# A grouped 1x1 convolution on one core: other ring sizes, slots of unequal size, a longer TensorE loop

## The chip, the core and the metric

The kernel runs on one core of one Trainium2 chip. The metric is device time in microseconds of one execution, the median of several runs; lower is better. A profiled execution gives a page and a trace, in which times count from the start of its span.

## The reference

The image has 512 x 512 pixels of 192 channels in bf16. The channels form 4 groups of 48, and each group is multiplied by a 48 x 48 matrix of its own, pixel by pixel (the window is 1 x 1, so there is no padding):

```python
xg = xp.reshape(B, H, W, G, Cg)                              # G = 4, Cg = 48
out = out + jnp.einsum('bhwgc,gcd->bhwgd', xg, w[0, 0])
return out.reshape(B, H, W, C)                               # C = 192
```

Input and output are 100.7 MB each, and every byte is moved once.

## The kernel before

**Columns and groups.** The 262,144 pixels are dealt to 128 partitions, 2,048 to each. One *column* is one pixel in each of the 128 partitions (384 bytes a partition). Four columns are a *group* (the `g` of the code), and there are 514 groups, 2 more than 512, because two short fields use fewer partitions. Two groups are a *pair*: 257 pairs.

**Fields.** `plan_fields` cuts the pixels into fields of consecutive pixels. In a full field (`FULL`) each of the 128 partitions holds one run of pixels. Two fields of 48 columns (`PARTIAL`, `UNEVEN`) are moved by five smaller transfers, two from SP or ACT and three from GpSimd, so that the DMA engines get unequal shares. In these fields 120 of the 128 rows are moved; in `UNEVEN` the first block also has 16 columns less. GpSimd issues small filler transfers (`filler`) ahead of two of its three.

**Rings.** Input lands in `ring`, 240 columns in three slots of 80. Results stand in `oring`, 280 columns, from which they are stored. `plan_pieces` lists the loads (pieces), at most a slot long; the first ones are `HEAD`, 8, 24 and 48 columns. `plan_stores` lists the stores, which end at the columns of `OGRID`, 72 or 68 columns apart, and get shorter at the end (`LATE_PART`, `LAST_PARTS`). A *unit* is one or more pieces that TensorE waits for together, at the first group of the unit.

**The work on a pair.** TensorE transposes the pair (12 transposes, L350) from `ring` to PSUM; VectorE copies it to one of `NXS` = 3 buffers `xT_sb` (L409); TensorE multiplies it by block-shaped weights (12 matmuls, L370); ScalarE copies each group to `oring` (L446) and issues the stores (L427). TensorE goes one pair ahead with its transposes: `step(pair)` is `transposes(pair + 1)`, then `matmuls(pair)`. Its program is unrolled in part: `loop_spans` finds a stretch of regular units, and a loop of 60 groups (30 pairs) runs 8 times; before it stand 9 pairs, after it 8.

**What orders the work.**
- SP goes through the pieces in order. Before a piece it waits until TensorE has transposed the groups whose columns the piece overwrites (`freed`, semaphore `t_done`), then it issues (L320). GpSimd does its parts of the two partial fields in the same way (L289 to L300), and tells TensorE when such a unit has landed.
- VectorE waits for the transposes of its pair and, because of its buffers, for the matmuls of `NXS` pairs before.
- ScalarE waits for the matmuls of its group; it issues a store when its last group is done; and before it writes columns of `oring` it waits for the landing of the store that read them before (`landed`, L420).

Of the kernel before, what the change touches and what calls it, by code (L numbers as in the profile page):

```python
# [1 line left out]

# [19 lines left out]
ESHIFT = 112  # L22
ECOLS = 272

BIG = 80
SLOTS = 3
RCOLS = SLOTS * BIG
OGRID = (72, 140, 212, 280)
OCOLS = OGRID[-1]
HEAD = (8, 24, 48)  # L30
LATE_COLS = 240
LATE_PART = 40
LAST_PARTS = (24, 20, 16, 8)
NXP = 4
NXS = 3
NOB = 4
NTOK = 6

FULL = (("sync", 0, 128, 128, 0),)

PARTIAL = (
    ("sync", 0, 16, 4, 0), ("sync", 32, 16, 4, 0),
    ("pool", 52, 44, 11, 0), ("pool", 20, 12, 3, 0), ("pool", 96, 32, 8, 0),
)
UNEVEN = (("sync", 0, 16, 4, 16), *PARTIAL[1:])
FRONT = ((6, ((48, PARTIAL), (32, FULL))), (11, ((48, UNEVEN), (32, FULL))))

FILL_ROWS = 5
FILL_BEFORE = (2, 3)


class Field:


    def __init__(self, cols, blocks, g0, pix):
        self.cols, self.g0, self.g1 = cols, g0, g0 + cols // 4
        self.full = blocks is FULL
        self.blocks = []
        for (queue, r0, rows, outer, less) in blocks:
            self.blocks.append((queue, r0, rows, outer, pix, cols - less))  # L60
            pix += rows * (cols - less)
        self.pix_end = pix
        assert cols % 4 == 0


class Piece:

    def __init__(self, i, field, c0, size):
        self.i, self.field = i, field
        self.c0, self.c1, self.size = c0, c0 + size, size  # L70
        self.g0, self.g1 = field.g0 + self.c0 // 4, field.g0 + self.c1 // 4
        self.at = 4 * self.g0 % RCOLS
        self.full, self.blocks = field.full, field.blocks
        assert size % 4 == 0 and self.at + size <= RCOLS

# [7 lines left out]

def plan_fields(npix):

    parts, head = [], sum(HEAD)
    for slots, special in FRONT:
        parts += [(head + BIG * slots, FULL), *special]
        head = 0
    cols = npix - sum((n - b[4]) * b[2] for n, blocks in parts for b in blocks)  # L90
    if cols < 128 * BIG:
        parts, cols = [], npix
    assert cols % 512 == 0
    fields, g, pix = [], 0, 0
    for n, blocks in [*parts, (cols // 128, FULL)]:
        fields.append(Field(n, blocks, g, pix))
        g, pix = fields[-1].g1, fields[-1].pix_end
    assert pix == npix
    return fields


def plan_pieces(fields):
    pieces = []
    for f in fields:
        first = [f.cols]
        if f.full:
            first = list(HEAD) if not f.g0 and sum(HEAD) <= f.cols else []
        c = 0
        while c < f.cols:
            n = first.pop(0) if first else min(BIG, f.cols - c)  # L110
            pieces.append(Piece(len(pieces), f, c, n))
            c += n
    return pieces


def plan_stores(fields):
    total = 4 * fields[-1].g1
    stores, at = [], 0
    for f in fields:
        c = 0  # L120
        if not f.full and at + f.cols > OCOLS:
            at = 0
        ends = []
        if f is fields[-1] and f.cols > LATE_COLS:
            ends = [f.cols - sum(LAST_PARTS[i:]) for i in range(len(LAST_PARTS))]
        while c < f.cols:
            if f.full:
                end = min([g for g in OGRID if g > at + 24] or [OCOLS]) - at + c
                if f.cols < BIG:
                    end = min(OCOLS - at + c, f.cols)  # L130
                if ends and c >= f.cols - LATE_COLS:
                    end = min(OCOLS - at, LATE_PART) + c
                end = min([end, f.cols] + [e for e in ends if e > c])
            else:
                end = f.cols
            stores.append(Store(f, c, end, at))
            c, at = end, (at + end - c) % OCOLS
    return stores


class Unit:


    def __init__(self, pieces):
        self.pieces, self.g0, self.g1 = pieces, pieces[0].g0, pieces[-1].g1
        self.slot = pieces[0].at // BIG
        self.regular = pieces[0].at % BIG == 0 and 4 * (self.g1 - self.g0) == BIG


def plan_units(pieces):  # L150
    units, rest = [], list(pieces)
    while rest:
        n = 1
        if rest[0].g0 and rest[0].at % BIG == 0:
            while n < len(rest) and rest[n].at % BIG:
                n += 1
        units.append(Unit(rest[:n]))
        rest = rest[n:]
    return units


def loop_spans(units):

    body, out, run = RCOLS // 4, [], []
    for u in units + [None]:
        if u and u.regular:
            run.append(u)
            continue
        if run:

            first = max((run[0].g0 - 1) // 2, 1)
            rounds = (run[-1].g1 - 2 * first - 2) // body
            if rounds > 1:
                out.append((first, body // 2, rounds))
        run = []
    return out


def bass_standalone__grouped__vision_kernel(nc, x, w, out):
# [11 lines left out]
    NG = pieces[-1].g1  # L191
    NP = (NG + 1) // 2
    LOOPS = loop_spans(units)
    assert all(RCOLS // 4 % n == 0 for n in (2 * NXS, 2 * NTOK, NXP))

# [4 lines left out]
    def groups(pair):  # L200
        return range(2 * pair, min(2 * pair + 2, NG))

    def transfers(ap, tile, part, queues):
        f, c0, c1, at = part.field, part.c0, part.c1, part.at
        for n, (queue, r0, rows, outer, pix, cols) in enumerate(f.blocks):
            if queue not in queues:
                continue
            px = ap[pix:pix + rows * cols, :]
            if f.full:
                view = px.rearrange("(p i) n -> p (i n)", p=rows)[:, c0 * C:c1 * C]  # L210
            else:
                assert (c0, c1) == (0, f.cols)
                view = px.rearrange("(c a i) n -> a c (i n)", a=outer, c=rows // outer)
            yield n, view, tile[r0:r0 + rows, at * C:(at + (c1 - c0 if f.full else cols)) * C]
# [12 lines left out]
    with ExitStack() as es:  # L227
        block = es.enter_context(nc.Block())
        ring = es.enter_context(nc.sbuf_tensor("ring", [128, RCOLS * C], BF16))
        oring = es.enter_context(nc.sbuf_tensor("oring", [128, OCOLS * C], BF16))  # L230
        xT_sb = [es.enter_context(nc.sbuf_tensor(f"xT_sb{i}", [128, 4 * UC], BF16)) for i in range(NXS)]
        ident = es.enter_context(nc.sbuf_tensor("ident", [128, 128], BF16))
# [7 lines left out]
        def sem(name):  # L240
            return es.enter_context(nc.semaphore(name))
# [6 lines left out]

        e_done = [sem(f"e_done{i}") for i in range(NTOK)]
        fa_done = [sem(f"fa_done{i}") for i in range(2 * NTOK)]  # L250
        fin = sem("fin")
# [3 lines left out]
        def columns(g):  # L255
            at = 4 * g % RCOLS
            return ring[:, at * C:(at + 4) * C]
# [11 lines left out]
        def _(gp):  # L269
# [12 lines left out]
            def filler():  # L282
                k = len(used)
                src = xf[0:2 * FILL_ROWS, 0:4].rearrange("(t p) n -> p t n", t=2)
                dst = fill[:, 8 * k:8 * k + 8].rearrange("p (t n) -> p t n", t=2)
                gp.dma_start(dst, src).then_inc(fill_sem[k], 16)  # L286
                used.append(k)

            for nth, u in enumerate(mixed):  # L289
                part = [p for p in u.pieces if not p.full]  # L290
                for p in part:
                    gp.wait_ge(t_done, freed(p))
                    for n, dram, sbuf in transfers(xf, ring, p, ("pool",)):
                        if n in FILL_BEFORE:
                            filler()
# [6 lines left out]
                for i, s in enumerate(stores):  # L302
                    if any(s.field is p.field for p in part):
                        for n, dram, sbuf in transfers(of, oring, s, ("pool",)):
                            if n in FILL_BEFORE:
                                filler()
# [16 lines left out]
        def _(pe):  # L323
# [12 lines left out]
            def transposes(pair):  # L336
                todo = []
                for g in groups(pair):
                    u = unit_of[g]
                    if g % 2 and pair:  # L340
                        pe.wait_ge(e_done[(pair - 1) % NTOK], 1)
                    if g == u.g0:
# [14 lines left out]
            def matmuls(pair):  # L357
                if pair + 1 == NP or len(groups(pair + 1)) < 2:
                    pe.wait_ge(e_done[pair % NTOK], 1)
                for g in groups(pair):  # L360
                    xs = xT_sb[pair % NXS][:, g % 2 * 2 * UC:(g % 2 + 1) * 2 * UC]
                    if g >= 2:
                        pe.wait_ge(fa_done[(g - 2) % (2 * NTOK)], 1)
                    last = None
# [35 lines left out]
        def _(dve):  # L400
            dve.wait_ge(wb_sem, 1)
            dve.tensor_copy(wt[:], o_ps[:, NOB - 1, 0:WCOLS]).then_inc(wc_sem, 1)  # L402
            for pair in range(NP):
                n = len(groups(pair))
                b0 = pair * 2 % NXP
                dve.wait_ge(t_done, pair + 1)
                if pair >= NXS:
                    dve.wait_ge(mm_done, 2 * (pair - NXS + 1))
                dve.tensor_copy(xT_sb[pair % NXS][:, 0:n * 2 * UC].rearrange("p (g c) -> p g c", g=n),  # L409
                                xT_ps[:, b0:b0 + n, 0:2 * UC]).then_inc(e_done[pair % NTOK], 1)  # L410
# [70 lines left out]
```

## Time and profile before

| | |
|---|---|
| median of 5 runs | 477.93 us (477.24 to 478.76) |
| the profiled execution | 477.8 us, span 476.1 us |
| PE busy, DVE busy, ACT busy | 90%, 52%, 82% of the span |
| bytes moved, mean rate | 201.57 MB, 423 GB/s |
| ScalarE's copy L446, VectorE's copy L409 | 801 ns x514, 958 ns x257 |
| SP's waits for TensorE (L320) | 397.9 us in 25 waits |
| ACT's waits for landed stores | 17.0 us in 8 waits |

The page cuts the span into 40 slices and gives each engine's busy share of a slice in tenths. The row DMA is the mean share of 16 DMA engines, and PEclk is the granted clock of TensorE in tenths. The chain is followed back from the last instruction, at each step to what released it. A row of the timeline has the start, the length, the engine, the line and, in brackets, the idle time before it with what ended it.

### The profile page before, as it was taken

To read this page: it belongs to the slowest core of one execution; us is meant where nothing else is said; L and a number is where in the kernel's file an instruction comes from. 1 tells how busy PE (TensorE), PEld (TensorE's weight loads), DVE (VectorE), ACT (ScalarE), POOL (GpSimd) and SP (SyncE) were. 2 spreads that over 40 slices of the span, in tenths; PEclk is the share of its full clock that TensorE was granted. 3 is DMA by queue.
4 is the path that set the end of the run, shared out by engine and by line. 5 is a ranking of instruction groups with operands and counts; after the bars stand their busy time and mean duration, and the time that the engine had idled before them with its cause. 6 is when DMAs were issued, how large, how long until landed. Compare 5 with 4: busy or idle time off the path is not lost.

```text
span 476.1 us, 13580 instructions
## 1 busy us (share of the span) xinstructions
PE 429.9 (90%) x6178; PEld 388.4 (82%) x6178; DVE 246.7 (52%) x258; ACT 388.5 (82%) x515; POOL 12.5 (3%) x28
## 2 busy tenths in 40 slices
PE   5999999999698999999997996899978969999991
PEld 4988889888697898888896896888878868988880
DVE  2555555555354555555553553555545535555550
ACT  2898899988587998988896885899878948988882
POOL 1000000200002000000000000200002000000000
PEclk9999999999999999999998998999999979999997
DMA  8999999999999999999999999999999999999997
GB/s 326 436 399 423 439 426 430 430 423 431 441 430 423 440 419 439 439 430 425 424 431 442 434 430 425 431 426 443 428 426 428 430 425 427 431 428 435 418 424 298
DMA packets 10674, 201.57 MB, mean 423 GB/s; under 512 B 2112, under 2 KB 2112, under 8 KB 2752
## 3 DMA queue, kind: packets, MB, share of 16 engines
q1 hardware_dynamic: 4320, 97.44, 48.0%
q10 hardware_dynamic: 5120, 97.42, 47.8%
q0 software_dynamic: 1216, 6.49, 3.3%
q8 instruction: 9, 0.15, 0.1%
q14 instruction: 9, 0.07, 0.0%
HBM read 100.68 MB, written 100.66 MB: 423 GB/s over the span
## 4 chain that ended last, share of the span: by engine, by line
PE 47%; DMA 39%; ACT 9%; issue 1%; another core or an unknown queue 1%; ACTq 1%; SPq 0%; POOLq 0%
DMA out_dram<-oring 30%; PE o_ps L370 27%; PE xT_ps L350 20%; DMA ring<-in_x_dram 9%; ACT oring L446 9%; ACTq L427 1%; SPq L320 0%; SPq L313 0%; ACTq L420 0%; POOLq L300 0%; POOLq L299 0%; ACTq L429 0%
## 5 line engine op out<-in xcount | busy, mean ns | idle before, releaser
L446 ACT CAST oring<-o_ps 128x768 bf16<-128x768 f32 x514 | 387.2, 801 | 77.7 <-PE o_ps L370 54.2
L409 DVE COPY xT_sb<-xT_ps 128x1536 bf16<-128x1536 bf16 x257 | 246.1, 958 | 214.1 <-PE xT_ps L350 214.1
L370 PE MATMUL o_ps<-wt,xT_sb 128*128 128x144 bf16 (+1 forms) x3084 | 289.2, 237 | 26.5 <-ACT oring L446 21.0
L370 PEld LDWEIGHTS o_ps<-wt,xT_sb 128*128 128x128 bf16 x3084 | 212.3, 99 | 65.0 <-ACT oring L446 55.9
L350 PE MATMUL xT_ps<-ident,ring 128*128 128x128 bf16 x3084 | 221.6, 222 | 6.7 <-POOLq L300 3.7
L350 PEld LDWEIGHTS xT_ps<-ident,ring 128*128 128x128 bf16 x3084 | 189.1, 99 | 9.5 <-POOLq L300 3.9
L286 POOL DMA_DIRECT2D fill<-in_x_dram x8 | 4.6, 573 | 349.1 <-PE xT_ps L350 234.5
L296 POOL DMA_DIRECT2D ring<-in_x_dram x6 | 3.3, 560 | 0.0
L307 POOL DMA_DIRECT2D out_dram<-oring x6 | 3.3, 555 | 0.0
L332 PE MATMUL o_ps<-w_sb,esel 48*128 48x48 bf16 x10 | 0.6, 210 | 2.8 <-DMA w_sb<-in_w_dram 2.8
L332 PEld LDWEIGHTS o_ps<-w_sb,esel 48*128 48x128 bf16 x10 | 0.5, 111 | 2.7 <-issue 2.7
L402 DVE CAST wt<-o_ps 128x480 bf16<-128x480 f32 x1 | 0.7, 657 | 3.3 <-PE o_ps L332 3.3
L446 ACT ACT_TABLE_LOAD x1 | 1.3, 1283 | 0.8 <-PEq L466 0.8
L273 POOL TENSOR_SCALAR_AFFINE_SELECT esel<-esel 48x272 bf16<-48x272 bf16 x1 | 0.4, 402 | 0.0
L270 POOL MEMSET esel<- 48x272 bf16 x1 | 0.3, 317 | 0.3 <-POOLq L466 0.3
L277 POOL TENSOR_SCALAR_AFFINE_SELECT ident<-ident 128x128 bf16<-128x128 bf16 x1 | 0.3, 283 | 0.0
L271 POOL MEMSET ident<- 128x128 bf16 x1 | 0.2, 197 | 0.0
L466 POOL MEMSET const-float32-0.0<- 128x1 f32 x1 | 0.1, 98 | 0.3 <-issue 0.3
L466 POOL MEMSET const-bfloat16-1.0<- 128x1 bf16 x1 | 0.1, 101 | 0.0
L466 POOL MEMSET const-uint8-127<- 128x1 uint8 x1 | 0.1, 101 | 0.0
L466 POOL MEMSET const-float32-1.0<- 128x1 f32 x1 | 0.1, 98 | 0.0
## 6 DMA issues: line engine op xcount, KB each, us to landing
ring<-in_x_dram SPq DMA_DIRECT2D x22, 3840.0 KB, 26.9
out_dram<-oring ACTq DMA_DIRECT2D x11, 3456.0 KB, 41.2
out_dram<-oring ACTq DMA_DIRECT2D x10, 3264.0 KB, 41.4
out_dram<-oring ACTq DMA_DIRECT2D x3, 1920.0 KB, 21.8
out_dram<-oring ACTq DMA_DIRECT2D x1, 3840.0 KB, 44.0
ring<-in_x_dram SPq DMA_DIRECT2D x2, 1536.0 KB, 31.4
out_dram<-oring ACTq DMA_DIRECT2D x2, 1536.0 KB, 41.9
out_dram<-oring ACTq DMA_DIRECT2D x1, 2880.0 KB, 39.0
```

Of the source, the lines that this page charges most:

```text
L273: gp.affine_select(out=esel[:], in_=esel[:], pattern=[[-1, ECOLS]], compare_op=AluOpType.is_equal, fill=0.0, base=ESHIFT, channel_multipli ...
L286: gp.dma_start(dst, src).then_inc(fill_sem[k], 16)
L296: gp.dma_start(sbuf, dram).then_inc(ld_sem[ld_key[p.i, n]], 16)
L307: gp.dma_start(dram, sbuf).then_inc(st_sem[i][n], 16)
L332: last = pe.matmul(o_ps[:, NOB - 1, col:col + CG], lhsT=esel[:, s0:s0 + 128], rhs=w_sb[:, g, :], start=True, stop=True, skip_group_check=True)
L350: last = pe.transpose(xT_ps[:, g % NXP, j * 128:(j + 1) * 128], xg[:, j * 128:(j + 1) * 128], ident[:])
L370: last = pe.matmul(o_ps[:, v % NOB, c0_:c1_], lhsT=xs[:, j * 128:(j + 1) * 128], rhs=wt[:, WOFF[tc]:WOFF[tc] + (c1_ - c0_)], start=(tc == ...
L402: dve.tensor_copy(wt[:], o_ps[:, NOB - 1, 0:WCOLS]).then_inc(wc_sem, 1)
L409: dve.tensor_copy(xT_sb[pair % NXS][:, 0:n * 2 * UC].rearrange("p (g c) -> p g c", g=n), xT_ps[:, b0:b0 + n, 0:2 * UC]).then_inc(e_done[pa ...
L427: act.dma_start(dram, sbuf).then_inc(st_sem[i][n], 16)
L446: act.copy(out_columns(g).rearrange("p (u c) -> p u c", u=2), o_ps[:, v % NOB:v % NOB + 2, 0:UC]).then_inc(fa_done[g % (2 * NTOK)] if g < ...
L466: nc = _bacc.Bacc("TRN2", target_bir_lowering=False, num_devices=1)
```

## The change

Six things change together.

1. The input ring has 256 columns in slots of 88, 84 and 84 (before 240, three of 80). A helper `slot_at` gives the slot of a column and the room to its end.
2. `xT_sb` has two buffers (before three), and there are eight semaphores of its kind (before six).
3. The output ring has 272 columns in stores of 68 (before 280, in turn 72 and 68). The sum of the three stays at 544 columns.
4. The head is 8, 24 and 56 columns (before 8, 24, 48); `LATE_PART` is 44 (before 40).
5. The partial fields come at groups 192 and 427 (before 140 and 380), and what follows them is no longer a field of 32 columns of its own.
6. The loop of TensorE has 64 groups (32 pairs). It runs 7 times, with 32 pairs before it and one after; the rest of the division stands mostly ahead of the loop.

```diff
-BIG = 80
-SLOTS = 3
-RCOLS = SLOTS * BIG
-OGRID = (72, 140, 212, 280)
+SLOT_COLS = (88, 84, 84)
+RCOLS = sum(SLOT_COLS)
+OGRID = (68, 136, 204, 272)
 OCOLS = OGRID[-1]
-HEAD = (8, 24, 48)
+HEAD = (8, 24, 56)
 LATE_COLS = 240
-LATE_PART = 40
+LATE_PART = 44
 LAST_PARTS = (24, 20, 16, 8)
 NXP = 4
-NXS = 3
+NXS = 2
 NOB = 4
-NTOK = 6
+NTOK = 8
...
-FRONT = ((6, ((48, PARTIAL), (32, FULL))), (11, ((48, UNEVEN), (32, FULL))))
+FRONT = ((RCOLS + 2 * RCOLS, 48, PARTIAL), (3 * RCOLS + 88 + 84 - 48, 48, UNEVEN))
...
+def slot_at(at):
+
+    for slot, end in enumerate(accumulate(SLOT_COLS)):
+        if at < end:
+            return slot, end - at
...
-            n = first.pop(0) if first else min(BIG, f.cols - c)
+            n = first.pop(0) if first else min(slot_at((4 * f.g0 + c) % RCOLS)[1], f.cols - c)
...
 class Unit:
-    def __init__(self, pieces):
+    def __init__(self, pieces, last):
         self.pieces, self.g0, self.g1 = pieces, pieces[0].g0, pieces[-1].g1
-        self.slot = pieces[0].at // BIG
-        self.regular = pieces[0].at % BIG == 0 and 4 * (self.g1 - self.g0) == BIG
+        self.slot, room = slot_at(pieces[0].at)
+        self.regular = room == SLOT_COLS[self.slot] and (last or 4 * (self.g1 - self.g0) == room)
...
-        if rest[0].g0 and rest[0].at % BIG == 0:
-            while n < len(rest) and rest[n].at % BIG:
+        if rest[0].g0:
+            slot, room = slot_at(rest[0].at)
+            while n < len(rest) and sum(p.size for p in rest[:n]) < room:
                 n += 1
-        units.append(Unit(rest[:n]))
+        units.append(Unit(rest[:n], n == len(rest)))
...
             first = max((run[0].g0 - 1) // 2, 1)
-            rounds = (run[-1].g1 - 2 * first - 2) // body
+            rounds, rest = divmod(run[-1].g1 - 2 * first - 2, body)
             if rounds > 1:
-                out.append((first, body // 2, rounds))
+                out.append((first + rest // 2, body // 2, rounds))
```

What the plans make of it, where the two differ:

| | before | after |
|---|---|---|
| units at the start (groups) | 0-1, 2-7, 8-19, 20-39 | 0-1, 2-21, 22-42 |
| pieces of the unit from group 2 | 24 | 24 and 56 |
| last pieces (columns) | 80, 80, 56 | 84, 84, 8 |
| loads from SP, stores planned | 30 pieces, 37 stores | 29 pieces, 37 stores |
| last stores (columns) | 80, 72, 68, 40, 40, 40, 20, 28, 24, 20, 16, 8 | 68, 8, 48, 80, 44, 24, 44, 40, 24, 20, 16, 8 |
| groups that write where an earlier store stood, late in the run | 470 over the store of 400-419 | 459 over the store of 391-407 |

More of the change, by code (lines that the diff above doesn't have):

```diff
@@ L1 @@
 from contextlib import ExitStack
+from itertools import accumulate
 import concourse.bass as bass
@@ L84, in plan_fields @@
 def plan_fields(npix):
[L86 to L89, printed above, removed]
+    parts = []
+    for n, special, blocks in FRONT:
+        parts += [(n, FULL), (special, blocks)]
     cols = npix - sum((n - b[4]) * b[2] for n, blocks in parts for b in blocks)
-    if cols < 128 * BIG:
+    if cols < 128 * RCOLS:
         parts, cols = [], npix
@@ L128, in plan_stores @@
                 end = min([g for g in OGRID if g > at + 24] or [OCOLS]) - at + c
-                if f.cols < BIG:
+                if f.cols < 80:
                     end = min(OCOLS - at + c, f.cols)
```

## The prediction

> **What bounds the kernel now.** I read the page from the DMA side first. Part 2 and part 3:
>
> ```profile
> DMA  8999999999999999999999999999999999999997
> DMA packets 10674, 201.57 MB, mean 423 GB/s; under 512 B 2112, under 2 KB 2112, under 8 KB 2752
> q1 hardware_dynamic: 4320, 97.44, 48.0%
> q10 hardware_dynamic: 5120, 97.42, 47.8%
> q0 software_dynamic: 1216, 6.49, 3.3%
> q8 instruction: 9, 0.15, 0.1%
> ```
>
> The reader is to see that loads (q1), stores (q10) and GpSimd's parts (q0) together fill 99% of the time of 16 engines. Every byte must move once each way; only the first and the last slice have room. So the kernel is bound by transfers, and a change of buffers can gain only at the two ends, but can lose wherever it starves the engines. The table of stretches shows the margin that compute has at the end (columns: stretch, length, busy us and count of PE, PEld, DVE, ACT, POOL, then PE clock, DMA share, GB/s):
>
> ```profile
> 380.00:400.00 20.00, 16.20 (x212) 15.17 (x211) 8.07 (x9) 13.08 (x18) 0.00 (x0) 0.83 1.00 423
> 400.00:430.00 30.00, 29.22 (x428) 26.07 (x425) 17.22 (x18) 26.25 (x36) 0.00 (x0) 1.00 1.01 430
> 450.00:467.00 17.00, 14.98 (x210) 12.73 (x207) 8.18 (x9) 15.08 (x20) 0.00 (x0) 1.00 1.00 423
> 467.00:476.00 9.00, 0.00 (x0) 0.00 (x0) 0.00 (x0) 0.03 (x1) 0.00 (x0) 0.66 0.63 263
> ```
>
> From 400 on compute runs without a rest and still is done only at 467, 9 us ahead of the end. The chain of work that ended last, and the timeline of ACT, give the last turn at which compute waited for the output ring:
>
> ```profile
> 385.60 44.00 DMA out_dram<-oring
> 429.68 1.51 ACT oring L446 x2
> ...
> 466.23 0.80 ACT oring L446
> ```
> ```profile
> 429.68 2.98 ACT L446 CAST oring<-o_ps 128x768 bf16<-128x768 f32 x4 [0.49 <-DMA out_dram<-oring]
> 467.06 0.34 ACTq L427 DMA_DIRECT2D out_dram<-oring  x1
> ```
>
> The copy at 429.68 is that of group 470 (44 copies of L446 stand from there to the end). It had waited 0.49 us for the store of groups 400 to 419, issued at 385.60, landed at 429.60. From there 44 groups took until 467.03: **0.849 us a group**. A group is 4 columns x 128 partitions x 384 B = 196,608 B each way; 1,028 such moves took from 2.2 to about 475, 0.460 us each, **0.92 us a group** for load and store. So while loads still run, compute (0.85) is a little faster than the transfers (0.92); once only stores are left (0.46), it is much slower, and eats into the stores that are queued.
>
> [...] the clock is 0.83 in the stretch 380 to 400, in which PE stood for some 5 us. [...] Here q8 brought 9 packets, 0.15 MB, in all 8 rounds of a loop of 1,440 matmul and weight-load instructions [...]: this loop was held.
>
> **The change part by part.**
>
> *Two buffers of transposed input, eight semaphores for six.* The copy L409 of pair p now waits for the matmuls of pair p-2. PE issues those ahead of the transposes of pair p, for which the copy waits anyway. Cost 0, covered by PE's order, which the change keeps. The semaphores cost nothing by themselves: no instruction per pair is added.
>
> *Loop of 64 groups.* 1,138 matmuls with as many weight loads stand in the program before, 1,570 after: [...] so 3 or 4 fetches more. q8's 0.1% of 16 x 476 us over 9 packets is about 0.85 us each: 3.4 us on one engine, 0.2 us in the mean. [...] I take +0.2; the ends are 0 (hidden in an engine that ends early) and the rival of a loop that isn't held, below.
>
> *Head of 8, 24, 56.* The new units put the pieces of 24 and 56 columns in one unit, so the first transposes of group 2 wait for both (before, for that of 24 alone: chain, DMA ring until 7.56, PE at 7.70). The piece of 48 landed 10.8 us after its issue at about 2.2, at 13.0; one of 56 lands 8 x 0.114 later, at 13.9. All that stands behind on PE, and DVE and ACT after it, starts **6.2 us later**. PE was cold until 12.6 and will be so until about 18. The first request after the head then comes late: SP issued it at 23.7 after 10 pairs; now after 11 pairs, 23.7 + 1.6 + 6.2 = 31.5, first bytes 1.0 later (as for the first load, 1.25 to 2.3). The head of 256 columns keeps the engines busy until about 3.3 + 256 x 0.114 = 32.5. So cover and need meet almost exactly: 0 to 1.5 us of empty engines, I take **0.4**. With 240 columns and no delay there were 7 us of cover. Later the delay is absorbed, as ACT would have waited for landings anyway.
>
> *Input ring of 256, slots of 88/84/84; partial pieces at groups 192 and 427.* Bytes and rate are the same; 29 loads for 30 and 37 stores as before are nothing. SP's waits (398 us, one per piece) stay hidden while three slots are queued; 240 to 256 columns makes that cover longer. The waits of SP's and POOL's queues move with the partial pieces and carry the same five transfers per field each way and the same eight fillers. No gain in the middle, since nothing is idle there. Four columns more read-ahead per slot means that loads run out sooner and the stage with stores alone begins earlier, which by the paces above costs cover at the end.
>
> *Output ring of 272, stores of 68.* A column is used again 68 groups later, not 70: ACT needs each landing 2 groups, 1.8 us, sooner. In the trace ACT waited 17.0 us in 8 such waits; they get longer by up to 1.8 us each. In the middle that is hidden by queued transfers. At the end it decides: the plan puts groups 459 to 469 on columns 204 to 247, where groups 391 to 407 stood. So the last gate now is at **group 459, with 55 groups behind it** (before: 470 with 44).
>
> When does it open? At 429.60 before, 420 groups of stores had landed, and (429.6 - 2.2)/0.460 = 929 moves were done, so 509 of loads. The same account gives 408 + 509 = 917, 424.0. Add 0.4 for the start. The partial piece now lies 19 groups behind this gate; the engines that carry GpSimd's rows then lag (in the trace the 16 parts of the store before the gate landed from 409.2 to 429.6), for which I add 0 to 3, taken 2: **426.4**. Then 55 x 0.849 = 46.7: last copy done at 473.1. [...] some 1.7 us lost; I take half, 0.8: **473.9**. The stores of 16 and 8 columns finish from there: the first is issued 1.2 us ahead, first bytes after 1.6 (467.06 to 468.64), 24 columns x 0.114 = 2.7, landing and end 0.9 (475.2 to 476.1): +4.0, span 477.9. Bound by transfers alone it would be 476.1 + 0.2 + 0.4 = 476.7. The later one holds: 477.9, against a span of 476.1. The profiled execution took 477.8, 1.7 over its span, and the median is 477.93: **477.9 + 1.7 = 479.6; taken 479.4**, as the trace's own execution stands 0.1 under the median and the lag is the softest term.
>
> **Rivals.**
> - *Transfers still set the end.* The gate opens at 424 and PE stays warm: compute ends at 471, hidden; span 476.7, time 478.3. For: the account without lag. Against: the later start and the partial piece close to the end. Within 0.2% (about 1 us, what a measurement can tell).
> - *Faster: the engines end more evenly.* Between 467 and 476 the DMA share is 0.63, 3.3 us idle in the mean, partly because the engines end up to 5 us apart. The partial pieces, which give some engines less, now come later (groups 192 and 427), so the last engine may end nearer to the mean: up to 2 us less, 476.2. It decides only if compute is done by about 470, so that the last bytes find a queue.
> - *The loop isn't held.* [...] Against: nothing shows that the limit is this near.
> - That the change does not do what it says is excluded for the buffers, as sizes and waits follow from the plan.
>
> **How the numbers follow.** Late compute at the end 0.57; transfers alone 0.20; evener end 0.17; loop not held 0.06. So slower 0.63, same 0.20, faster 0.17. Late compute by itself spans 478.9 (no lag, cold restart) to 483.5 (gate at 429.5 with a cold restart). The range 476.8 to 483.5 takes in the transfers' case and part of the faster one.
>
> **What would show it.** PE's second batch of transposes at about 13.9 and the second load after the head near 31.5; a wait of ACT for a landing at group 459 near 426, 55 copies after it; last store issued near 474 (467.1 before); DMA share under 1 in the 10 us ahead of that; q8 with 12 or 13 packets. It is wrong if the last issue stays below 470, or if q8 shows dozens of packets.

## The result, and the profile after

The changed kernel takes **481.54 us** (median of 27 runs, 477.61 to 483.99), the kernel before in the same jobs 478.18 us (48 runs). The ratio is **1.0065, interval 1.005 to 1.008**: slower by some 3.1 us. (The ratios here and below are not exactly the quotients of the medians.) The runs of the changed kernel spread over 6 us; those of the kernel before lie mostly between 477 and 479. The profiled execution of the changed kernel is one of its quick ones, 478.74 us with a span of 477.0 us, so the size of the loss can't be read from it alone; a second profile (experiment e4) took 480.63 us.

The page of after, the row of the DMA share and the rows of the queues:

```profile
DMA  8999999999999999999999999999999999999997
q1 hardware_dynamic: 4176, 97.44, 48.0%
q10 hardware_dynamic: 5120, 97.42, 47.8%
q8 instruction: 12, 0.20, 0.1%
```

Loads and stores are the same bytes at the same share. q8 brought 12 packets for 9. In the trace the last of the 12 landed at 122.2 us and none came in the six rounds of the loop after the first: the loop of 64 groups was held. What this page hides is seen in the table of stretches (columns as in the prediction: stretch, length, PE, PEld, DVE, ACT, POOL, PE clock, DMA share, GB/s). The kernel before:

```profile
24.00:40.00 16.00, 15.65 (x235) 14.26 (x234) 9.32 (x10) 14.55 (x21) 0.00 (x0) 1.00 0.98 396
445.00:470.00 25.00, 19.86 (x282) 17.32 (x282) 10.75 (x12) 19.54 (x26) 0.00 (x0) 1.00 0.99 418
```

The first profile of after:

```profile
24.00:40.00 16.00, 15.63 (x235) 14.17 (x232) 8.82 (x11) 14.28 (x20) 0.00 (x0) 1.00 1.00 398
445.00:470.00 25.00, 24.26 (x352) 21.45 (x350) 14.27 (x15) 22.08 (x30) 0.00 (x0) 1.00 0.94 402
```

Between 445 and 470 the engines are 94% busy for 99%, while PE works without a rest (24.26 us of 25): the last stores now wait for compute. The timeline of the same profile shows the two turns that matter, the start of TensorE and the gates of the output ring. A *gate* is a group at which ACT must wait for the landing of an earlier store before it may write the same columns:

```profile
4.76 1.44 PE L358 MATMUL xT_ps<-ident,ring 128*128 128x128 bf16 x12 [1.39 <-DMA ring<-in_x_dram]
14.21 1.44 PE L358 MATMUL xT_ps<-ident,ring 128*128 128x128 bf16 x12 [8.01 <-DMA ring<-in_x_dram]
...
425.00 0.80 ACT L454 CAST oring<-o_ps 128x768 bf16<-128x768 f32 x1 [2.46 <-DMA out_dram<-oring]
440.86 0.80 ACT L454 CAST oring<-o_ps 128x768 bf16<-128x768 f32 x1 [1.84 <-DMA out_dram<-oring]
472.95 0.34 ACTq L435 DMA_DIRECT2D out_dram<-oring  x1
```

PE's second batch starts at 14.21 (7.70 before). ACT stops at group 459 until 425.00 and again at group 476 until 440.86; after each it continues at its own pace, and the last store is issued at 472.95, **5.9 us later** than the 467.06 of before. The chain of waits in the stretch 400 to 477 names the second stop as the last one:

```profile
391.52 49.27 DMA out_dram<-oring
...
472.12 0.80 ACT oring L454
```

**How far the end hangs on compute** can be read from two numbers of each profile, the issue of the last store and the end of the span. Where transfers set the end, the queues still hold work at that issue; where compute does, nothing but the last short stores is left.

| kernel (profile) | last store issued | end of span | between |
|---|---|---|---|
| before | 467.06 | 476.1 | 9.0 |
| after, first profile | 472.95 | 477.0 | 4.1 |
| after again (e4) | 475.36 | 478.9 | 3.5 |
| after, late stores halved (e1) | 474.57 | 478.1 | 3.5 |
| after, head in two units (e2) | 473.58 | 477.7 | 4.1 |
| after, both (e5) | 473.41 | 477.2 | 3.8 |
| after, loop of six rounds (e7) | 477.30 | 480.8 | 3.5 |
| after, loop of six and 30 transposes (e8) | 477.49 | 481.0 | 3.5 |
| after, loop of six and 80 transposes (e9) | 475.90 | 479.7 | 3.8 |
| before, output ring 272 (e3) | 467.29 | 476.9 | 9.6 |
| before, head joined (e6) | 469.15 | 477.7 | 8.6 |
| before, output ring 288 (e10) | 467.93 | 475.1 | 7.2 |
| before, longer program (e11) | 470.16 | 477.2 | 7.0 |

Every version of after ends 3.5 to 4.1 us after its last store, every version of before 7.0 us or more. In after the wait for compute shows in the time; in before it is covered, that is, hidden behind transfers that are still queued (a DMA share of 0.63 from 467 to 476). This would also explain why after spreads more, since what shifts the last gate by a microsecond shifts its end. That is argued and not shown: the runs of e3, whose end is covered in its profile, spread over 4 us too.

### The profile page after: what moved, and what is told of

It is laid out like the page before. It is cut to its first block, busy times and chain, and to the rows that moved or that the text cites. A ratio compares the mean times of both kernels' runs of the same rounds, so it can differ in the third digit from the quotient of the medians.

```text
span 477.0 us, 13587 instructions
## 1 busy us (share of the span) xinstructions
PE 428.6 (90%) x6178; PEld 386.9 (81%) x6178; DVE 246.7 (52%) x258; ACT 388.2 (81%) x515; POOL 12.5 (3%) x28
## 4 chain that ended last, share of the span: by engine, by line
DMA 51%; PE 39%; ACT 6%; issue 1%; ACTq 1%; SPq 0%
DMA out_dram<-oring 49%; PE o_ps L378 23%; PE xT_ps L358 17%; ACT oring L454 6%; DMA ring<-in_x_dram 2%; ACTq L435 1%; SPq L328 0%; SPq L321 0%; ACTq L428 0%; ACTq L437 0%
```

## The experiments

Two accounts stood against each other. **The gate**: only the end counts, through the output ring of 272 and the late landing of the stores of groups 391 to 424. **Two places**: the start, where the joined head delays everything by 6 us, costs by itself. All ratios are to the kernel before on the same chip.

**e4, the changed kernel once more**, unaltered, for a second profile.

> The kernel after unchanged, to see beside the others on the same chip what its usual execution looks like: ratio 1.005 to 1.008. The first profile of it was of a quick execution (478.7 against a median of 481.5). Theory of the gate: in a slower one ScalarE's stops at groups 459 and 476 end later by the same microseconds as the execution is longer, and the DMA share in the last 30 us falls. Rival loop: more packets of instructions than 12. Rival head: the difference stands already at 40 us.

Measured: 482.0 us, ratio 1.0079 (1.0056 to 1.0101); the profiled execution 480.63 us. Its stretches and its gate:

```profile
24.00:40.00 16.00, 15.74 (x234) 14.16 (x232) 9.36 (x10) 14.24 (x20) 0.00 (x0) 1.00 0.94 371
445.00:470.00 25.00, 24.39 (x358) 21.79 (x356) 13.65 (x16) 22.08 (x30) 0.00 (x0) 1.00 0.92 391
```
```profile
427.32 0.80 ACT L454 CAST oring<-o_ps 128x768 bf16<-128x768 f32 x1 [3.44 <-DMA out_dram<-oring]
428.17 0.59 PE L378 MATMUL o_ps<-wt,xT_sb 128*128 128x144 bf16 x6 [3.57 <-ACT oring L454]
430.88 1.49 PE L358 MATMUL xT_ps<-ident,ring 128*128 128x128 bf16 x12
475.36 0.34 ACTq L435 DMA_DIRECT2D out_dram<-oring  x1
```

Against the first profile the gate at group 459 opens 2.3 us later, PE stands for 3.57 us instead of 2.44 and, a microsecond after it comes back, drops to half clock for about 3.4 us (12 transposes took 0.90 us at 428.60, 1.49 at 430.88 and 0.83 at 433.23; the clock was 0.86 in the 10 us from 422), and the last store is issued 2.4 us later. There is no later stop. From 427.32 to the end of the last copy (475.33) are 48.0 us for 55 groups, 1.3 more than 55 x 0.849. And the start shows a loss that the first profile didn't have in this stretch: 371 GB/s for 398 between 24 and 40. (Over the first 100 us both profiles of after show a loss; see e6.)

**e1, the stores from group 391 on cut in half**, so that the gates at 459 and 476 wait for shorter stores. The plan has three stores more (40 for 37), not four as the expectation says.

```diff
+FINE = (36, 68, 104, 136, 172, 204, 240, 272)
+FINE_FROM = 391
-                end = min([g for g in OGRID if g > at + 24] or [OCOLS]) - at + c
+                grid = FINE if f.g0 + c // 4 >= FINE_FROM else OGRID
+                end = min([g for g in grid if g > at + 24] or [OCOLS]) - at + c
```

> The kernel after, with one edit: from group 391 on the output columns are stored in halves (36 and 32 columns instead of 68), so that the last copies of ScalarE wait for the landing of half a store. Same bytes, rings, loop, head and partial pieces; four stores more. Theory of the gate (the output ring's last landings hold ScalarE back, compute ends too late to be hidden): the columns that groups 459 and 476 write come free some 4 to 7 us earlier, ScalarE's stops there shrink from 3.3 and 2.7 us to under 1, the last store is issued near 469 to 470, and the time falls to that of the kernel before, within 1 us (ratio 0.999 to 1.002). Rival head (the start 6 us late is never made up): no change from the kernel after, ratio 1.006. Rival loop and instruction fetches: no change, 1.006. Rival engines' spread (the partial pieces' new places leave the DMA engines uneven): at most half is won, 1.003.

Measured: 479.98 us, ratio 1.0045 (1.003 to 1.006). The stop at group 459 is gone, but a new one stands at group 468, in the timeline of ACT:

```profile
433.90 2.28 ACT L457 CAST oring<-o_ps 128x768 bf16<-128x768 f32 x3 [3.94 <-DMA out_dram<-oring]
```

From 433.90 the 46 groups left take 40.6 us, and the last store goes out at 474.57. The finer stores only moved the gate; 0.0020 of the 0.0065 was won back, about a third (0.0034 against e4 of the same job; for all gains I use the 27 runs, the more careful figure). The gate account, which asked for all of it, falls short.

**e2, the head of after in two units again**: the pieces of 24 and 56 columns no longer share one wait; everything else stays.

```diff
-        if rest[0].g0:
+        if rest[0].g0 and rest[0].at in (0, *accumulate(SLOT_COLS)):
```

> The kernel after, with one edit: the pieces of 24 and 56 columns at the start are units of their own again, so TensorE's second batch of transposes waits for the 24 columns alone and compute starts about 6 us earlier. Theory of the gate: the late groups wait for landings whose time the transfers set, not the start; the time stays that of the kernel after, ratio 1.005 to 1.007, and the stops of ScalarE in the first 200 us grow by what the start gained. Rival head: the whole loss goes, ratio 1.000, or at least the 0.4 us of empty engines near 31 us.

Measured: 479.28 us, ratio 1.0025 (1.0008 to 1.0043). The gate account had no change here; some 0.4%, 1.9 us, came back (0.0040, and 0.0054 against e4). SP's first request after the head goes out at 24.8, for 31.3 in after. The table of stretches of this kernel:

```profile
24.00:40.00 16.00, 15.63 (x235) 14.20 (x233) 8.82 (x11) 14.23 (x20) 0.00 (x0) 1.00 0.98 405
445.00:470.00 25.00, 24.38 (x356) 21.65 (x354) 13.94 (x16) 22.08 (x30) 0.00 (x0) 1.00 0.92 389
```

The start moves 405 GB/s; the end is as starved as before this edit, with a stop at group 476 until 441.49. So the gain was not made at the last gate. That the loss lies at the start is tested by e6, in a kernel whose end is covered.

**e5, e1 and e2 together.**

> The kernel after with the edits of the first two experiments together: the head's pieces of 24 and 56 in units of their own, and stores in halves from group 391 on. Alone they brought 1.0025 and 1.0045, from 1.0065 to 1.0079. Theory of two independent losses (empty engines near 31 us from the late start, and compute that ends too late to be hidden): the gains add, ratio 0.999 to 1.001, and the DMA share stays at 1 until 470. Rival of one loss (both edits only move the same last stop of ScalarE): no better than the better one alone, 1.002 to 1.003. Rival that something else in the change costs too (loop, fetches, partial pieces): it stays at 1.001 to 1.002 or above.

Measured: 479.12 us, ratio 1.0015 (1.0001 to 1.003). In the two stretches:

```profile
24.00:40.00 16.00, 15.74 (x233) 14.11 (x231) 9.15 (x10) 14.23 (x20) 0.00 (x0) 1.00 0.99 404
445.00:470.00 25.00, 24.06 (x348) 21.23 (x346) 13.82 (x15) 21.77 (x30) 0.00 (x0) 1.00 0.95 406
```

The head gives 0.0040 in e2, the finer stores 0.0020 in e1, together 0.0050. Within the intervals this fits gains that add; but it can't be told from e2 alone either (1.0025, 1.0008 to 1.0043), so the rival that both edits move the same stop is not excluded by this run. About 0.0015 stays, and the end still stands 3.8 us behind the last store: a stop of 3.95 us, at 433.2, was left.

**e6, the joined head alone, in the kernel before.**

```diff
-        n = 1
+        n = 2 if rest[0].g0 == 2 else 1
```

> The kernel before, with one part of the change alone: the pieces of 24 and 48 columns at the start are one unit, so TensorE's second batch of transposes waits for both, some 5.4 us later than before. Rings, head sizes, loop and partial pieces as before. With 240 columns of head and loads at about 29 us the engines run empty near 30.5 us only if the first request comes later than that: 23.7 + 5.4 = 29.1, first bytes at about 30.1. Theory of the cover: 0 to 0.5 us, ratio 0.999 to 1.002, as the last stop and what follows it are the transfers' and the margin at the end is kept. Rival head (the late start costs by itself, wherever it is): the loss that the first of these experiments took away, ratio 1.003 to 1.005.

Measured: 479.6 us, ratio 1.0039 (1.0024 to 1.0055). The same 0.4% as e2 gave back, in a kernel whose end is covered (8.6 us between last store and end):

```profile
24.00:40.00 16.00, 15.62 (x233) 14.04 (x231) 9.05 (x11) 14.56 (x20) 0.00 (x0) 1.00 0.96 370
445.00:470.00 25.00, 21.79 (x307) 18.89 (x306) 12.11 (x13) 21.20 (x29) 0.00 (x0) 0.99 0.99 420
```

370 GB/s for 396 over 16 us are 0.42 MB; at the 430 GB/s of the middle (40 to 120 in before) this is **1.0 us** of transfers lost between 24 and 40. By the busy share alone (0.96 for 0.98) it would be 0.3 us; why the engines moved less while they counted as busy is open. The request after the head went out at 29.6 (before: 23.7). A longer stretch shows the loss more fully. The first 100 us of before, of the first profile of after, and of e6:

```profile
0.00:100.00 100.00, 92.74 (x1330) 84.08 (x1330) 53.33 (x56) 81.84 (x109) 4.25 (x13) 1.00 0.99 415
0.00:100.00 100.00, 86.28 (x1241) 78.03 (x1242) 49.97 (x53) 76.53 (x102) 1.31 (x8) 1.00 0.99 413
0.00:100.00 100.00, 87.30 (x1245) 79.27 (x1246) 50.05 (x53) 76.79 (x102) 4.25 (x13) 1.00 0.98 410
```

Of the other profiles, those with the head in two units have 414 to 416 GB/s here (e2, e3, e5, e10, e11), those with the joined head 410 to 412 (e1, e4 and e7 to e9). At 430 GB/s the difference to before is about 1.2 us in e6, 0.9 in e4 and 0.5 in the first profile of after. The span of e6 is 1.6 us longer than that of before; the other 0.4 us has no place here.

**e3, the output ring of 272 alone, in the kernel before.**

```diff
-OGRID = (72, 140, 212, 280)
+OGRID = (68, 136, 204, 272)
```

> The kernel before, with one part of the change alone: output ring of 272 columns in stores of 68 (280 before, 72 and 68). Three slots of 80, three transposed buffers, head, loop and partial pieces as before. Theory of the gate, if the size of the output ring by itself makes it: landings are needed 2 groups sooner, compute ends 1 to 2 us later, part of which is hidden: ratio 1.001 to 1.004. If it is where the last gate falls (which group writes over which store) rather than the size: about 1.000 to 1.002. Rivals head, loop, partial pieces: 1.000, as none of them is in it.

Measured: 479.17 us, ratio 1.0024 (1.0008 to 1.0039). ACT's waits for landings grow from 17.0 us in 8 to:

```profile
ACT oring L446 <- DMA out_dram<-oring: 20.1, 10, 7.6
```

But the last store goes out at 467.29, as before, with 9.6 us of queued transfers behind it. With the old fields the smaller ring does not starve the end of this profile; its 0.24% has no place in it. This kernel has one gate in common with after, group 476 over the store of groups 408 to 424, and here it opened 5.6 us earlier than the 440.86 of after, though the store was issued only 1.0 us earlier (after: 391.52):

```profile
390.48 0.34 ACTq L427 DMA_DIRECT2D out_dram<-oring  x1
435.24 0.80 ACT L446 CAST oring<-o_ps 128x768 bf16<-128x768 f32 x1 [1.07 <-DMA out_dram<-oring]
```

So an output ring of 272 columns does not by itself make this gate late. The head doesn't either, since e2 has it at 441.49. Of what differs between e2 and e3, the longer input ring and the new places of the partial fields (one of them at groups 427 to 438, just behind that store) are the candidates that stand out; neither was tried alone.

**e10, an output ring of 288 and two transposed buffers, in the kernel before**, the sum of buffers again 544 with the input ring left at 240 columns.

```diff
-OGRID = (72, 140, 212, 280)
+OGRID = (72, 144, 216, 288)
-NXS = 3
+NXS = 2
```

> A version that may beat both: the kernel before with two transposed buffers (as in the change) and the 8 columns that this frees given to the output ring: 288 columns, stores of 72. Input ring, head, loop and partial pieces as before. Theory of the gate and of transfers as the bound: the two buffers cost nothing, landings are needed 2 groups later, so no stop near the end; but compute was hidden at the end already, so the time is that of the kernel before, ratio 0.998 to 1.001, with the slow tail of its times (up to 482) thinned. Rival (the third transposed buffer was of use): over 1.002.

Measured: 477.7 us, ratio 0.9995 (0.9987 to 1.0003). Giving up the third transposed buffer and gaining 8 columns of output ring cost and gain nothing together. That each of them by itself is worth nothing is not shown, as one could hide the other.

**e11, the kernel before with its loop two rounds shorter** and those 60 groups unrolled: the price of instruction fetches.

```diff
-                out.append((first, body // 2, rounds))
+                out.append((first + body // 2, body // 2, rounds - 2))
```

> The kernel before, with its TensorE loop run 6 times in place of 8 and 30 pairs more unrolled on each side of it: the same work, and some 12 packets of instructions more (about 21 for 9), half of them early and half late. Everything else as before. Theory that a fetch costs only the time that it takes from one of the 16 engines: 12 x 0.85 / 16 = 0.6 us, up to 1 us where the late ones fall on the engine that ends last: ratio 1.001 to 1.002. If fetches stall TensorE: [...] the ratio is over 1.003. If they are free: 1.000.

Measured: 478.8 us, ratio 1.0013 (0.9996 to 1.003). On its page:

```profile
q8 instruction: 20, 0.33, 0.2%
```

Eleven packets more for about 0.6 us, with an interval that includes no cost at all: as an estimate some 0.05 us a packet, 0.15 us for the three that the change added, and perhaps nothing. (The six packets that e7 adds to after, below, cost nothing that can be measured.)

**e7, e8, e9: the cold restart at the gate.** e7 is after with six rounds of the loop, so that pair 230 stands in unrolled code; e8 and e9 are e7 with 30 and with 80 transposes of the identity ahead of the matmuls of that pair, which only keep PE working while ACT is stopped.

```diff
-                out.append((first + rest // 2, body // 2, rounds))
+                out.append((first + rest // 2, body // 2, rounds - 1))
+WARM_PAIR = 230
+            def keep_warm():
+                for _ in range(30):
+                    pe.transpose(xT_ps[:, 0, 768:896], ident[:], ident[:])
...
+                if pair == WARM_PAIR:
+                    keep_warm()
                 matmuls(pair)
```

> The kernel after with the TensorE loop run 6 times and the last 33 pairs unrolled: a control for the next run, and a test of instruction fetches, as some 6 more packets of 16 KB are fetched, all in the last 60 us. Theory that fetches cost only what they take from the engines (0.85 us each on one engine, 0.05 in the mean, but late, and on the slowest engine all of it): ratio as the kernel after or up to 0.002 more, 1.006 to 1.010. Rival (a fetch stalls TensorE): [...] ratio over 1.010.

> The same as the run before it, and 30 transposes of the identity (some 1.7 us of PE) into unused columns of PSUM between the transposes of pair 231 and the matmuls of pair 230, where TensorE stops for ScalarE's wait at group 459. They fill part of a stop that is there anyway[...]. Theory of the cold restart ([...] the first profile, without that, was 2 to 3 us quicker than the median): 1 to 1.7 us less than the run before it, ratio lower by 0.002 to 0.0035, and no stretch of half clock between 425 and 440. Rival (the gate's time alone decides): the same as the run before, or up to 1 us longer where the stop was shorter than the filling.

> The run with 30 transposes as filling, now with 80 (4.4 us of PE at full clock). With 30, PE still stood 4.6 us at the gate of group 459, and ran 6.8 us at half clock after it, as without filling (6.3 us). With 80 about 1.9 us of standing are left[...]. Theory of the cold restart: no half clock between 425 and 445, the 55 groups behind the gate go at 0.85 us each, the last store is issued about 3 us sooner (half of 6.8) and the ratio falls from 1.0064 to about 1.001 to 1.003. Rival (the gate's time alone decides, a cold PE is hidden by ScalarE): no change from 1.006. Where an execution has only a short stop, the filling costs up to 2 us.

Measured: e7 481.24 us, 1.0064 (1.0048 to 1.0079), with 18 packets on q8; e8 481.51 us, 1.0066 (1.0045 to 1.0087); e9 480.32 us, 1.0061 (1.004 to 1.0082). The first stretch and the gate of e7:

```profile
422.00:432.00 10.00, 3.74 (x39) 3.50 (x37) 1.56 (x2) 2.40 (x4) 0.00 (x0) 0.79 0.99 421
```
```profile
428.24 0.80 ACT L454 CAST oring<-o_ps 128x768 bf16<-128x768 f32 x1 [6.14 <-DMA out_dram<-oring]
429.10 0.98 PE L378 MATMUL o_ps<-wt,xT_sb 128*128 128x144 bf16 x6 [6.26 <-ACT oring L454]
```

PE stood for 6.26 us, then worked at half clock for some 5.5 us (12 transposes took 1.49 us until 434.2, and 0.83 us after that); the 55 groups took 49.0 us, 2.3 more than at full pace. The 30 transposes of e8 were used up long before the gate opened, and PE stood 4.61 us all the same, so e8 tells nothing. In e9 the clock held:

```profile
422.00:432.00 10.00, 9.68 (x157) 9.06 (x155) 3.61 (x4) 4.93 (x8) 0.00 (x0) 1.00 0.99 420
```
```profile
430.30 2.98 ACT L461 CAST oring<-o_ps 128x768 bf16<-128x768 f32 x4 [3.35 <-PE o_ps L379]
```

but there ACT, whose gate had opened at 426.14, waited 3.35 us for PE to get through the filling. The last store goes out 1.4 us earlier than in e7, and the medians cannot be told apart. What a warm restart would be worth stays open.

## Why the prediction was right, and where its terms were off

**The end (right mechanism, gate early).** Compute takes the place of transfers as the bound of the end, as forecast: DMA share 0.92 to 0.94 ahead of 470 with PE busy throughout, last store at 472.95 and 475.36 ("near 474"), and 4.1 and 3.5 us from there to the end (the step said 4.0). The gate at group 459 was put at 426.4; it opened at 425.00, 427.32 and, in e7, 428.24. That it opens late is a matter of more than the output ring, to which the step gave the leading part: e3 has that ring, and there the store of groups 408 to 424 had landed 5.6 us earlier than in after. The lag that the step put on the partial piece behind the gate is the better candidate, but no run tried it alone. In the first profile a gate that the prediction had not listed came after it, at group 476 over the store of groups 408 to 424: 440.86 + 38 x 0.849 = 473.1, and the last copy was done at 472.92. So the pace of 0.849 a group holds, and the term that carries the spread is the landing of one store. The added lag, "0 to 3, taken 2", was for the quick executions too high and for the slower ones, e4 and e7, 0.9 and 1.8 us too low.

**The cold restart (half of 1.7 taken).** At this gate it was not half but nothing after a stop of 2.44 us, 1.3 us of lost pace after 3.57, 2.3 after 6.26. When a stop brings half clock is not shown, and the 0.8 us were the author's estimate; a short stretch of half clock in before cost twice that, some 1.7 us (a clock of 0.86 in the 12 us from 248, 0.87 in the 13 us from 280). The length of the stop alone does not tell. In the first profile of after, PE stood for 2.98 us until 176.11 and then had a clock of 1.00 for the next 10 us; later it stood for only 2.50 us and then ran at a clock of 0.52 for 3.5 us:

```profile
392.35 0.59 PE L378 MATMUL o_ps<-wt,xT_sb 128*128 128x144 bf16 x6 [2.50 <-ACT oring L454]
393.00:396.50 3.50, 3.50 (x35) 3.45 (x33) 0.96 (x1) 2.15 (x3) 0.00 (x0) 0.52 0.97 418
```

So the measurement decides. The stop of "some 5 us" that the prediction saw between 380 and 400 in the kernel before lasted 3.74 us (the clock was 0.50 from 386.4 to 390.0):

```profile
386.43 1.78 PE L370 MATMUL o_ps<-wt,xT_sb 128*128 128x144 bf16 x12 [3.74 <-ACT oring L446]
```

**The head (0.4 taken, about 1.9 measured).** This is the term that was mis-sized. The times were right: PE at 14.21 for 13.9, the end of its slow start (12 transposes took 1.44 us at 14.21, 1.14 at 17.05, 0.89 at 18.85) for "about 18", the request at 31.3 for 31.5. The step put the loss at "0 to 1.5 us of empty engines"; e2 and e6 both give about 0.4% of 478 us, 1.9 us (the interval of e6 is 1.1 to 2.6 us). The traces place a part of it in the first 100 us: 1.2 us in e6, 0.9 in e4, 0.5 in the first profile of after, none in e2. The step counted only engines with nothing to do, and by the busy share these are not all of the loss; the rest of the 1.9 us is not located. That ACT would later absorb the delay did not hold: e6 was slower though its end was covered.

**The fetches (0.2 taken).** The 12 packets are as forecast, and e11's estimate of 0.05 us each agrees, with an interval that includes no cost. The count can be had from before as an estimate: 9 packets for the 2,276 matmuls and weight loads of its program are one for about 253, so the 3,140 of after ask for 12.4. The loop of after has 1,536 of them in a round, and with all 12 packets in by 122.2 us, none was fetched again in the six later rounds. How large a loop would still be held is not shown. **Two transposed buffers (0)** agree with e10, which has them together with a larger output ring.

**The sum.** 479.4 was forecast and 481.54 came. Of the 2.1 us between, about 1.5 is the head (1.9 for 0.4). How it reaches the end is not shown: in e4 the gate was 0.9 us later than forecast, but in e2, where the head is mended, the gate at 476 opened no earlier than in after (441.49 for 440.86). The restart adds 0.5 in e4 and 1.5 in e7. These are single profiles, of 480.63 and 482.54 us, on both sides of the median; the split is no finer than that. The direction did not hang on the head: of the 1.5 us by which the forecast lay above the kernel before, about 1.1 was late compute, and e2, without the joined head and with its end as starved, is still 0.0025, 1.2 us, slower (0.4 to 2.1). That these two figures meet so closely is in part luck, since e2 keeps the rest of the change as well. One sum of the working is off: late compute with "no lag, cold restart" gives 424.4 + 46.7 + 1.7 + 4.0 + 1.7 = 478.5, not 478.9; nothing hangs on it.

**The rivals.** Transfers alone: refuted by the share of 0.92 to 0.94 and the last issue above 470. A more even end: it needed compute done by about 470, which no profile of after shows. The loop that isn't held: refuted by q8.

**Still open:** 0.7 us or more of the head's price, what makes the gate at group 476 late, the place of the 0.24% of e3, the 0.15% left in e5, the worth of a warm restart, and the new places of the partial fields, which no run tried by themselves. Of all these kernels e10 has the lowest median, 477.7 us, and it ties with the kernel before.

## What to carry to other kernels

In a kernel bound by transfers, read the time between the issue of the last store and the end of the span: as long as it is well above what the last short stores need, compute is covered (7.0 us or more in the versions of before), and when it falls to that, a late gate can show in the time (3.5 to 4.1 us in those of after). List all gates of the output ring behind the last loads, not only the one that came last in the profile, since shortening one made the next one hold (a stop of 3.94 us in e1). Do not join the first loads under one wait: a start of compute 6 us later came back as 1.9 us in the time although the DMA share was 0.98 in e6 and 0.99 in after over the first 100 us.

## What the runs showed of the hardware

- One store doesn't land at one moment. In after the 16 parts of the store of groups 408 to 424 landed from 425.8 to 440.8, and the gate waits for the last. Behind a partial field the parts split: in before, all 16 parts of a store landed from 81.1 to 84.1 us, but of the store that landed at 151.7, after GpSimd's loads of 92 to 121 us, four parts landed from 140.0 to 140.9 and twelve from 149.3 on.
- About one in sixteen of the large store packets was slower than the others: in before, some 85 of the 1,408 packets of 27,648 bytes took 1.06 us or more, and most of the others 1.03 us. Whether these ran on one engine, the trace does not say.
- An instruction fetch of 16 KB took about 0.94 us on its engine (9 packets in before, 12 in after).
- While GpSimd's transfers of one field ran (153 to 184 us in before), its queue moved 88 packets of 18 KB, and the two hardware queues 239 and 240 packets. Its largest parts, of 792 KB, took 18.7 us (loads) and 20.2 us (stores) from issue to landing.
- A stop of PE of 2.50 us (after, until 392.35) was followed by 3.4 us at half clock (0.52 from 393.0 to 396.5), while one of 2.98 us (until 176.11) and one of 2.44 us (until 425.85) were not (1.00 from 176.1 to 186 and from 426.0 to 433.0).
